# A spectral filter and a dense layer in one kernel: six rows of x by another way, the order of the first loads, three buffers, new constants

## The chip, the cores and the metric

The kernel runs on one core of a Trainium2 chip. A core has a matrix engine (TensorE, PE; its weight loads are listed as PEld), a vector engine (VectorE, DVE), a scalar engine (ScalarE, ACT), a general engine (GpSimd, POOL), and a queue engine that only issues transfers (SyncE, SP). Each works through its own queue of instructions in order and waits for others by semaphores. All transfers run on 16 DMA engines that the queues share. A transfer issued by GpSimd may change the type on the way (here fp32 to fp16); one issued by SP doesn't here. The metric is the device time of one launch in microseconds; the median of five runs is quoted.

## What is computed

```python
X = np.fft.rfft(x, axis=1)                     # x: 8 x 3008 x 256
Y = X * (filt_r + 1j * filt_i)[None, :, :]
y = np.fft.irfft(Y, n=3008, axis=1)            # the same shape
h = y.reshape(24064, 256) @ w_in               # w_in: 256 x 2048
out = np.maximum(0.01 * h, h) @ w_out          # w_out: 2048 x 256
```

A circular filter along the sequence of each batch, then two dense layers with a leaky ReLU between them. Inputs and output are fp32; matrices work in fp16 with fp32 sums.

## The kernel before

The transform of length 3008 is split as 94 x 32. `x_sb` has position n1 (94) on partitions and n2 (32) beside the 256 channels; a "row" of x below is one n2, that is 94 x 256 values. Four steps follow for each batch:

- stage 1 multiplies by `fwd1` (94-point transforms, in `small_sb`),
- stage 2 multiplies by `f2_sb`, one 128 x 128 matrix for each of 24 column groups c, and the result is multiplied with the filter (`fa_sb`, `fb_sb`),
- stage a multiplies by the inverse matrices in `small_sb`,
- stage b multiplies by `i1_sb` and leaves `yt`, channels on partitions and tokens along the row.

Between stages 1 and 2, and a and b, the data is turned. **Batch 0** does this on chip, by DVE transposes: `t1` (L376 to L379, four of them, big0 to big1) and `t2` (big2 to big0). **Batches 1 to 7** write it to DRAM (`dz1`, `dz2`) and read it back turned, on SP's queue.

Batch 0 is the start of the kernel; its order is written out by hand in the string `FIRST` (L458), one step at a time, and each engine takes its own instructions from that order. The steps:

- `warm n`: n matmuls on a zero tile (`idle`), whose result nobody uses.
- `s1p _ n0 n b`: stage 1 of n rows from row n0 into PSUM bank b; `s1e _ n0 n e`: that bank into `big[0]`, by ACT (A) or DVE (D). A bank is filled again only when it has been emptied.
- `s2p hf c n i b`: stage 2 of n column groups from c, for half hf of the channels and component i. Its product with the filter is `s2d` on DVE straight from PSUM, or `s2a` (ACT copies four groups to a spare fp32 buffer) and `s2m` (GpSimd multiplies that). Eight of the 4-group pieces go by GpSimd, the rest by DVE.
- `sap` and `sae` (ACT): stage a and its eviction; `sbp` and `sbe`: stage b and its eviction to `yt`.
- `i1`: a DVE memset of two elements of `i1_sb`, then the SP load of the whole tile. The load waits for the memset, so that it is issued when DVE has come to this place.
- `x`: GpSimd loads x of batch 1 in two halves, with w_out between them.

Ahead of that string stand the first transfers (L205 to L217). SP: `small_sb`, and thirds 1 and 0 of `f2_sb` (column groups 8 to 15, and 0 to 7; 256 KB each). GpSimd, casting to fp16: x of batch 0 in parts of 10, 10, 8 and 4 rows; the filters' first half of channels (four transfers); third 2 of f2; the filters' second half; w_in.

After batch 0 a planner sets the order. Time is counted in slots: a chunk of 512 tokens takes SL = 8 slots, its 16 first-layer products (`moe1`, L502) stand 0.5 slots apart, and the second layer of the chunk before (`plain`, L627, for three chunks, then the seven-product form at L566) lies between them. Work of the next batches is put in at times given by `PLANS`: start and spacing of stage 1 (L250), of stages 2 (L299) and a (L321) with a lag, of stage b (L342), and of the loads of x; two groups are at least `GAP` = 0.6 slots apart. These stages now have two PSUM banks between them (L486 takes the third away), so that a group waits until the one two before it has been evicted.

In stage 2 of batches 1 to 7 (`s2_group`) DVE makes two fp32 products, p1 (L311) and p2 (L308); two SP transfers swap the halves of p2 into p3, and GpSimd adds p1 and p3 (L314). For every second group of batch 1 DVE writes p3 itself (L305, L306). p1, p2 and p3 come from the pool `scr` with two buffers each; the spare buffers of batch 0 are the same ones. `AFTER` gives the delays in slots at which dependent instructions are put into their queues, `TWICE` the times of six DVE copies that make `fb_sb` and the doubled `fa_sb` (L660 to L662), `F2T` that of a load of other matrices into `f2_sb`, `SUMS` those of DVE sums for the seven-product form, `REST` those of six stage-b groups of batch 0 that are left over, `DUE` and `LEAD` limits for stage b and for the reads of turned data. In batch 1, of four stage-1 groups DVE evicts three and ACT the fourth (L642).

Of the kernel before, what the change touches and what calls it, by code (L numbers as in the profile page):

```python
# [75 lines left out]
def kernel(  # L76
# [9 lines left out]
    nc = tc.nc  # L86
    B, N, D = x.shape
# [25 lines left out]
    PLANS = (
# [14 lines left out]
    f2_sb = cpool.tile([P, NC, P], FP16, name="f2_sb")  # L128
# [10 lines left out]

    gtp = ctx.enter_context(tc.tile_pool(name="gtp", bufs=2))  # L140
    drp = ctx.enter_context(tc.tile_pool(name="drp", bufs=1, space=bass.MemoryType.DRAM))
    scrp = ctx.enter_context(tc.tile_pool(name="scr", bufs=2))
    ypp = ctx.enter_context(tc.tile_pool(name="ypp", bufs=4))
    outp = ctx.enter_context(tc.tile_pool(name="outst", bufs=4))
    psp = ctx.enter_context(tc.tile_pool(name="psp", bufs=1, space=bass.MemoryType.PSUM))
# [42 lines left out]
    def x_load(b, n0=0, nn=N2, d0=0, dn=D):  # L188

        for lo, cnt in ((0, R1),) if b + 1 < B else ((0, 64), (64, N1 - 64)):  # L190
            nc.gpsimd.dma_start(
                x_sb[lo : lo + cnt, ds(n0, nn), ds(d0, dn)],
                bass.AP(tensor=x.tensor, offset=x.offset + (b * N + lo * N2 + n0) * D + d0,
                        ap=[[N2 * D, cnt], [D, nn], [1, dn]]))
# [50 lines left out]
    def s1_group(b, g, copy):  # L245
        def go():
# [109 lines left out]
    engine = {"A": act, "D": dve}  # L356
# [91 lines left out]
        nc.vector.memset(i1_sb[:, 0, 0:2], 0.0)  # L448
        nc.sync.dma_start(i1_sb[:], i1_d.ap())

    def load_x():

        x_load(1, 0, N2 // 2)
        nc.gpsimd.dma_start(w_out_sb[:], moe_w_out.rearrange("(ct p) d -> p ct d", p=P))
# [3 lines left out]
    FIRST = """  # L458
        warm 18, s1p 0 0 2 b0, s1e 0 0 2 A, s1p 0 2 4 b3, s1p 0 6 4 b4, s1e 0 2 4 D, warm 4, s1p 0 16 4 b3,
        s1e 0 16 4 D, s1p 0 10 2 b1, s1e 0 6 4 A, s1p 0 12 4 b4, s1e 0 10 2 A, warm 2, s1p 0 24 2 b2,  # L460
        s1e 0 12 4 A, s1e 0 24 2 D, s1p 0 20 4 b3, s1e 0 20 4 A, s1p 0 26 2 b0, s1p 0 28 2 b1,
        s1p 0 30 2 b2, s1e 0 26 2 D, s1e 0 28 2 A, s1e 0 30 2 D, t1 1, t1 0, warm 14, s2p 0 0 4 0 b0,
        s2p 0 0 4 1 b1, s2p 0 16 4 0 b2, t1 2, t1 3, s2a 0 0 4 0, s2m 0 0 4 0, s2a 0 0 4 1, s2p 0 16 4 1 b0,
        s2p 0 8 8 0 b4, s2p 0 8 8 1 b3, s2a 0 16 4 0, s2m 0 16 4 0, s2a 0 16 4 1, s2m 0 16 4 1,
        s2p 0 4 4 0 b1, s2d 0 8 8 0, s2p 0 20 4 1 b2, s2d 0 8 8 1, i1, s2d 0 4 4 0, s2p 0 4 4 1 b0,
        s2p 1 8 8 0 b4, s2d 0 4 4 1, warm 1, s2p 1 8 8 1 b3, s2a 1 8 8 0, s2m 0 0 4 1, sap 0 8 b1,
        s2a 1 12 8 0, s2p 1 16 8 0 b4, s2d 0 20 4 1, sap 0 16 b0, s2m 1 12 8 0, x, s2a 1 8 8 1, s2m 1 8 8 1,
        s2d 1 16 8 0, sae 0 8 A, s2a 1 12 8 1, sae 0 16 A, s2p 0 20 4 0 b2, sap 0 4 b1, s2m 1 12 8 1,
        s2p 1 16 8 1 b3, sap 0 0 b0, s2p 1 0 8 1 b4, s2d 0 20 4 0, s2d 1 16 8 1, sae 0 4 A, s2m 1 8 8 0,
        sae 0 0 A, sap 0 20 b1, s2d 1 0 8 1, sap 0 12 b2, s2p 1 0 8 0 b3, sap 1 16 b0, sae 0 20 A,  # L470
        sae 0 12 A, sap 1 12 b1, s2d 1 0 8 0, sap 1 20 b2, t2 0, sap 1 8 b4, t2 1, sae 1 16 A, sap 1 4 b0,
        sap 1 0 b3, sae 1 12 A, warm 5, sbp 0 1 b1, sae 1 20 A, sae 1 8 A, sbp 0 4 b2, sae 1 4 A, sae 1 0 A,
        t2 3, sbp 0 5 b4, sbe 0 1 A, sbp 0 2 b0, t2 2, sbe 0 4 A, sbp 0 6 b3, sbe 0 5 A, sbp 0 7 b1,
        sbp 0 0 b2, sbp 0 3 b4, sbe 0 6 A, sbp 1 1 b3, sbe 0 0 D, sbe 0 2 A, sbp 1 0 b0, sbe 0 3 A,
        sbe 0 7 A, sbe 1 1 D, sbe 1 0 A
    """
# [180 lines left out]
    for i in range(2):  # L657
        k1s = ts(i, NC // 2)
        for n, f in enumerate((
                lambda v=k1s: nc.vector.tensor_scalar(fb_sb[64:P, v], fa_sb[64:P, v], -1.0, None, AL.mult),  # L660
                lambda v=k1s: dve(fb_sb[0:64, v], fa_sb[64:P, v]),
                lambda v=k1s: dve(fa_sb[64:P, v], fa_sb[0:64, v]))):  # L662
# [24 lines left out]
    while queue:  # L687
        time, n, stage, b, g, f = heapq.heappop(queue)
# [16 lines left out]
    for ci in range(NCHUNK + 1):  # L705
# [45 lines left out]
```

## Time and profile before

| what | us |
|---|---|
| median of five runs | 752.99 |
| all five | 752.58, 752.68, 752.99, 754.4, 755.68 |
| the profiled execution | 754.46 |
| its span | 752.7 |
| PE busy in the span | 738.9 (98%) |
| ACT, DVE, POOL busy | 559.0, 499.8, 163.5 |
| first product of the dense layers (L502) starts | 36.45 |
| last part of x for batch 0 is waited for until | 13.1 |
| first DVE transpose starts | 14.76 |

The profile has the program on one time axis that begins with the span. The granted clock of PE is full throughout (0.999). A line of the chain of waits has a start, a length, and who worked. A line of the timeline has a start, a length, engine, line, operation, result and operands with shapes, the count, and in brackets how long the engine had been idle before and what ended that. "SPq" is SP issuing a transfer; its moving of data comes later and is told by the packet records: queue, start, duration and bytes of each. A matmul's end is modelled, so steps between starts are the better measure of PE.

The 16 DMA engines are busy for nine tenths or more from about 2 us until 48 us; GpSimd's queue carries 7.47 MB of the 12.21 MB in the first 60 us.

### The profile page before, as it was taken

Reading aid. Unit: us, or ns where it says so; the run is one execution under the profiler, and the core shown is the slowest. Engines: PE = TensorE matmul, PEld = TensorE weight load, DVE = VectorE, ACT = ScalarE, POOL = GpSimd, SP = SyncE. Lnnn points to the kernel's source line nnn. Section 1 sums busy time; section 2 is a strip of 40 time slices with the busy share of each in tenths; the row PEclk is TensorE's granted clock in tenths of the full one; section 3 lists DMA queues with packets and bytes.
Section 4 is the critical chain, followed back from the end, with each engine's and each line's share of the span. In section 5 each row is a group of like instructions: output and inputs, shape, how many; then the busy total and the mean of one; then the engine's idle time right before and its main releaser. Section 6 shows DMA issues by size and latency. Waiting matters only on the chain.

```text
span 752.7 us, 19384 instructions
## 1 busy us (share of the span) xinstructions
PE 738.9 (98%) x8016; PEld 528.8 (70%) x8016; DVE 499.8 (66%) x683; ACT 559.0 (74%) x755; POOL 163.5 (22%) x169
## 2 busy tenths in 40 slices
PE   8999999999999999999999999999999999999997
PEld 3555667767777777877778777787777777777775
DVE  5886645777667776667666756776677576465565
ACT  3675797788878777787778787887777777777662
POOL 5503330342222221221133222212212210000000
PEclk9999999999999999999999999999999999999999
DMA  9985788887886567556676555544554333111011
GB/s 189 228 220 157 181 201 235 208 186 192 228 205 161 129 189 208 133 154 153 190 177 170 146 169 168 148 132 126 145 156 119 107 107 103 52 54 54 29 52 62
DMA packets 119688, 113.34 MB, mean 151 GB/s; under 512 B 16352, under 2 KB 92768, under 8 KB 119408
## 3 DMA queue, kind: packets, MB, share of 16 engines
q1 hardware_dynamic: 104447, 95.36, 42.3%
q0 software_dynamic: 14864, 16.49, 15.9%
q8 instruction: 62, 1.02, 0.6%
q10 hardware_dynamic: 289, 0.26, 0.1%
q14 instruction: 26, 0.21, 0.1%
HBM read 57.51 MB, written 50.33 MB: 143 GB/s over the span
## 4 chain that ended last, share of the span: by engine, by line
PE 92%; DMA 4%; DVE 1%; POOL 1%; issue 1%; ACT 0%; SPq 0%; DVEq 0%; ACTq 0%; POOLq 0%
PE ph L502 42%; PE po_ps L566 18%; PE pf L566 18%; PE pf L250 3%; PE pf L342 3%; PE pf L321 2%; PE pf L299 2%; DMA f_sb<-fwd_const 1%; PE po_ps L627 1%; PE pf L627 1%; DMA dz<-big 1%; DMA x_sb<-in_x_dram 1%; DMA p_b_g<-p_b_g 1%; PE pf L433 0%; POOL prod L396 0%
## 5 line engine op out<-in xcount | busy, mean ns | idle before, releaser
L507 ACT ACTIVATE gt_c<-ph 128x1024 f16<-128x1024 f32 x376 | 385.4, 1025 | 135.0 <-PE ph L502 124.3
L502 PE MATMUL ph<-yt,w_in_sb 128*128 128x512 f16 (+7 forms) x1728 | 447.6, 352 | 0.4 <-DVE yt L332 0.4
L566 PEld LDWEIGHTS <-gt_c 128*128 128x128 f16 x2800 | 202.1, 98 | 91.1
L314 POOL TENSOR_TENSOR y_b_g<-p_b_g,p_b_g 128x512 f16<-128x512 f32 x84 | 115.3, 1373 | 418.9 <-DMA p_b_g<-p_b_g 221.4
L566 PEld LDWEIGHTS <-big 128*128 128x128 f16 x2128 | 151.2, 98 | 61.6 <-issue 0.2
L502 PEld LDWEIGHTS <-w_in_sb 128*128 128x128 f16 x1728 | 137.4, 98 | 20.9 <-issue 1.8
L308 DVE TENSOR_TENSOR p_b_g<-pf,fb_sb 128x512 f32<-128x512 f32 x78 | 53.7, 688 | 32.7 <-PE pf L299 15.6
L566 PE MATMUL po_ps<-wt_sb,gt_c 128*128 128x128 f16 x704 | 70.1, 219 | 0.0
L566 PE MATMUL pf<-wt_sb,gt_c 128*128 128x128 f16 x688 | 68.5, 220 | 0.0
L566 PE MATMUL pf<-w_out_sb,gt_c 128*128 128x128 f16 x720 | 68.0, 220 | 0.0
L566 PE MATMUL po_ps<-wt_sb,big 128*128 128x128 f16 x720 | 67.5, 219 | 0.0
L566 PE MATMUL pf<-wt_sb,big 128*128 128x128 f16 x704 | 67.3, 219 | 0.0
L253 ACT CAST big<-pf 128x512 f16<-128x512 f32 x100 | 58.3, 588 | 11.9 <-PE pf L250 10.5
L566 PE MATMUL po_ps<-w_out_sb,gt_c 128*128 128x128 f16 x688 | 66.1, 220 | 0.0
L332 ACT CAST yt<-pf 128x376 f16<-128x376 f32 x120 | 56.4, 473 | 12.3 <-PE pf L342 9.0
L539 DVE TENSOR_TENSOR big<-gt_c 128x2048 f16<-128x2048 f16 (+1 forms) x46 | 58.2, 1266 | 0.1
L311 DVE TENSOR_TENSOR p_b_g<-pf,fa_sb 128x512 f32<-128x512 f32 x84 | 57.3, 682 | 1.4 <-POOL y_b_g L314 1.2
L539 DVE TENSOR_TENSOR gt_c<-gt_c 128x2048 f16<-128x2048 f16 x43 | 54.8, 1275 | 1.0
L539 DVE TENSOR_TENSOR big<-gt_c,big 128x2048 f16<-128x2048 f16 (+1 forms) x45 | 54.7, 1216 | 0.0
L539 DVE TENSOR_TENSOR big<-big,gt_c 128x2048 f16<-128x2048 f16 (+1 forms) x45 | 54.5, 1211 | 0.1
L323 ACT CAST big<-pf 128x512 f16<-128x512 f32 x84 | 49.0, 584 | 5.8 <-PE pf L321 4.1
L250 PE MATMUL pf<-x_sb,small_sb 94*128 94x512 f16 x112 | 42.7, 382 | 0.8 <-DVE big L253 0.8
(85 smaller groups left out, 618.4 us busy)
## 6 DMA issues: line engine op xcount, KB each, us to landing
dz<-big SPq DMA_DIRECT2D x98, 256.0 KB
p_b_g<-p_b_g SPq DMA_DIRECT2D x156, 128.0 KB
out_dram<-ost_c_h SPq DMA_DIRECT2D x119, 128.0 KB
big<-dz SPq DMA_DIRECT2D x42, 256.0 KB
big<-dz SPq DMA_DIRECT2D x56, 192.0 KB
x_sb<-in_x_dram POOLq DMA_DIRECT2D x41, 192.0 KB, 4.3
x_sb<-in_x_dram POOLq DMA_DIRECT2D x2, 768.0 KB, 12.2
w_in_sb<-in_moe_w_in_dram POOLq DMA_DIRECT2D x1, 1024.0 KB, 13.2
```

What stands on the lines that cost most here:

```text
L250: nc.tensor.matmul(ps, fwd1[:N1], x_sb[:N1, ds(2 * g, 2), :], start=True, stop=True)
L253: copy(st[:, ds(2 * (g % 2), 2), :], ps)
L308: nc.vector.tensor_tensor(p2[:], ps, fb, AL.mult)
L311: nc.vector.tensor_tensor(p1[:], ps, fa, AL.mult)
L314: ("y", b, g), lambda: nc.gpsimd.tensor_tensor(y1[:], p1[:], p3[:], AL.add)))
L323: nc.scalar.copy(st2[h % 4][:, ds(2 * (g % 2), 2), :], ps)
L332: copy(yv, ps.rearrange("p c a -> p a c"))
L342: nc.tensor.matmul(ps[:, j, :], z2[h % 4][:K4, j, ts(dt, P)], i1_sb[:K4, 4 * h + j, :], start=True, stop=True)
L502: nc.tensor.matmul(ph[:, j, ds(t - ci * CH, e - t)], w_in_sb[:, dt, ts(ct, P)], yt[:, dt, ds(t % N, e - t)], start=(dt == 0), stop=(dt == ...
L507: nc.scalar.activation(gts[ci][:, ds(2 * g, 2), :], ph, AF.Lrelu)
L539: nc.vector.tensor_tensor(*(v[:, ds(c0, n)] for v in (o, i0, i1)), op)
L566: nc.tensor.matmul(po[:, t], a()[:, c, ts(t, P)], w[:, c, :], start=(c == 0), stop=(c == NCH - 1))
```

## The change

- SP's first transfers are `small_sb` and then six rows of x in fp32, into the memory of `big[1]`, which is otherwise first written by `t1`. Two copies at the start of `FIRST` (`xc 0 4 A`, `xc 4 2 D`) round them to fp16 into `x_sb`. GpSimd loads the other 26 rows in parts of 10, 10 and 6.
- Third 0 of f2 is GpSimd's, behind x and ahead of the filters. Thirds 1 and 2 become steps `f2 1` and `f2 2`: a DVE memset and an SP load, as `i1` is; they stand among the evictions of stage 1 and behind the first transpose.
- `x` is split in `x 0`, `x 1` and `w_out`, in this order, later among GpSimd's products.
- The order of all steps of `FIRST` is another one, with other banks and another division between DVE, ACT and GpSimd (the numbers of pieces for each are the same in stage 2).
- The pool `scr` has three buffers for each of p1, p2, p3.
- Most constants of the planner are others.

```diff
-    SUMS = (0.09, 1.59, 2.35, 4)
-    REST = (5.37, 14.61, 8.86, 10.48, 23.53, 20.72)
-    DUE = (3.52, 0.66)
-    TWICE = (1.43, 1.84)
-    F2T = 3.24
-    LEAD = (3.85, 7.37)
-    AFTER = (0.53, 0.8, 1.33, 3.17, 0.39, 0.52)
+    SUMS = (0.05, 0.99, 2.69, 4.18)
+    REST = (4.12, 14.62, 8.89, 9.51, 23.97, 20.76)
+    DUE = (3.59, 0.63)
+    TWICE = (2.2, 2.35)
+    F2T = 3.43
+    LEAD = (3.63, 7.37)
+    AFTER = (0.53, 0.86, 1.77, 3.86, 0.39, 0.52)
...
-        (0.68, 0.31, 12.95, 0.9, 4.35, 38.33, 2.78, 7.78, 1.61),
-        (12.19, 1.53, 42.87, 2.62, 7.4, 85.59, 2.85, 16.13, 2.12),
-        (40.7, 1.73, 77.28, 3.57, 5.62, 130.03, 2.65, -0.23, 2.52),
-        (63.95, 2.85, 119.86, 3.87, 7.04, 177.42, 2.92, 12.93, 2.24),
+        (0.68, 0.42, 12.95, 0.9, 4.25, 38.32, 2.79, 7.58, 1.59),
+        (12.21, 1.53, 43.08, 2.51, 7.4, 85.59, 2.85, 16.73, 2.23),
+        (40.7, 1.74, 76.94, 3.44, 5.42, 128.19, 2.64, 0.06, 2.61),
+        (64.12, 2.86, 119.86, 3.87, 7.04, 177.42, 2.92, 13.96, 2.21),
...
-    scrp = ctx.enter_context(tc.tile_pool(name="scr", bufs=2))
+    scrp = ctx.enter_context(tc.tile_pool(name="scr", bufs=3))
...
+    EARLY = 6
+    x_early = big[1][:].bitcast(FP32)[:, : EARLY * D].rearrange("p (n d) -> p n d", n=EARLY)
     nc.sync.dma_start(small_sb[:], small_d.ap())
-    for i in (1, 0):
-        nc.sync.dma_start(f2_sb[:, ts(i, NC // FP), :], f2_d.ap()[i])
-    first_parts = ((0, 10), (10, 10), (20, 8), (28, 4))
-    for n0, nn in first_parts:
+    nc.sync.dma_start(x_early[:R1], bass.AP(tensor=x.tensor, offset=x.offset, ap=[[N2 * D, R1], [D, EARLY], [1, D]]))
+    for n0, nn in ((6, 10), (16, 10), (26, 6)):
         x_load(0, n0, nn)
+    nc.gpsimd.dma_start(f2_sb[:, : NC // FP, :], f2_d.ap()[0])
     for hf in range(2):
 
         filt_load(0, filt_r, hf * DH, DH)
         filt_load(64, filt_i, hf * DH, DH)
-        if hf == 0:
-            nc.gpsimd.dma_start(f2_sb[:, ts(2, NC // FP), :], f2_d.ap()[2])
...
+    def load_f2(i):
+
+        nc.vector.memset(f2_sb[:, i * NC // FP, 0:2], 0.0)
+        nc.sync.dma_start(f2_sb[:, ts(i, NC // FP), :], f2_d.ap()[i])
...
-        x_load(1, 0, N2 // 2)
+    def load_x(half):
+        x_load(1, half * N2 // 2, N2 // 2)
+        issued.add(("x", 1, 0))
+
+    def load_w_out():
         nc.gpsimd.dma_start(w_out_sb[:], moe_w_out.rearrange("(ct p) d -> p ct d", p=P))
-        x_load(1, N2 // 2, N2 // 2)
-        issued.add(("x", 1, 0))
+
+    def round_x(n0, n, e):
+        engine[e](x_sb[:N1, ds(n0, n), :], x_early[:N1, ds(n0, n), :])
...
+        xc 0 4 A, xc 4 2 D, warm 18, s1p 0 0 4 b3, s1p 0 4 2 b0, warm 3, s1p 0 14 2 b1, s1e 0 4 2 D,
+        s1e 0 0 4 A, s1p 0 10 4 b4, s1e 0 10 4 A, s1p 0 6 4 b3, s1e 0 14 2 D, warm 4, s1p 0 20 4 b4,
+        s1e 0 6 4 D, s1p 0 16 4 b3, s1e 0 16 4 A, s1p 0 26 2 b2, s1p 0 24 2 b0, s1e 0 24 2 A, f2 1,
+        s1e 0 20 4 D, s1p 0 28 2 b1, s1p 0 30 2 b4, s1e 0 26 2 D, s1e 0 30 2 A, s1e 0 28 2 D, t1 0, f2 2, t1 1,
+        warm 14, s2p 0 0 4 0 b3, s2p 0 0 4 1 b2, warm 2, s2p 0 8 4 1 b0, s2a 0 0 4 0, s2a 0 0 4 1, t1 3,
+        s2p 0 12 4 1 b4, t1 2, s2d 0 8 4 1, s2p 0 12 4 0 b1, s2p 0 16 8 0 b3, s2m 0 0 4 0, s2m 0 0 4 1,
+        s2d 0 16 8 0, s2a 0 12 4 1, s2p 0 8 4 0 b2, s2p 1 16 8 0 b4, s2p 0 4 4 1 b0, s2a 0 12 4 0, s2d 0 8 4 0,
...
+        x 0, s2m 1 16 8 0, sae 1 20 A, s2m 1 16 8 1, x 1, w_out, sae 1 12 A, sae 1 8 A, sap 1 16 b3,
+        sae 1 16 A, sap 1 4 b2, t2 1, sae 1 4 A, sap 1 0 b4, t2 0, sae 1 0 A, warm 4, sbp 0 1 b1, sbp 0 4 b0,
...
```

More of the change, by code (lines that the diff above doesn't have):

```diff
@@ L449, in load_i1 @@
         nc.sync.dma_start(i1_sb[:], i1_d.ap())
-    def load_x():
-        x_load(1, 0, N2 // 2)
+    def load_f2(i):
[5 more added lines that the diff above has]
+    def load_w_out():
         nc.gpsimd.dma_start(w_out_sb[:], moe_w_out.rearrange("(ct p) d -> p ct d", p=P))
-        x_load(1, N2 // 2, N2 // 2)
-        issued.add(("x", 1, 0))
+    def round_x(n0, n, e):
+        engine[e](x_sb[:N1, ds(n0, n), :], x_early[:N1, ds(n0, n), :])
@@ L458 @@
     FIRST = """
[L459 to L473, printed above, removed]
@@ L474 @@
-        sbp 0 0 b2, sbp 0 3 b4, sbe 0 6 A, sbp 1 1 b3, sbe 0 0 D, sbe 0 2 A, sbp 1 0 b0, sbe 0 3 A,
-        sbe 0 7 A, sbe 1 1 D, sbe 1 0 A
+        xc 0 4 A, xc 4 2 D, warm 18, s1p 0 0 4 b3, s1p 0 4 2 b0, warm 3, s1p 0 14 2 b1, s1e 0 4 2 D,
+        s1e 0 0 4 A, s1p 0 10 4 b4, s1e 0 10 4 A, s1p 0 6 4 b3, s1e 0 14 2 D, warm 4, s1p 0 20 4 b4,
+        s1e 0 6 4 D, s1p 0 16 4 b3, s1e 0 16 4 A, s1p 0 26 2 b2, s1p 0 24 2 b0, s1e 0 24 2 A, f2 1,
+        s1e 0 20 4 D, s1p 0 28 2 b1, s1p 0 30 2 b4, s1e 0 26 2 D, s1e 0 30 2 A, s1e 0 28 2 D, t1 0, f2 2, t1 1,
@@ new lines @@
+        warm 14, s2p 0 0 4 0 b3, s2p 0 0 4 1 b2, warm 2, s2p 0 8 4 1 b0, s2a 0 0 4 0, s2a 0 0 4 1, t1 3,
+        s2p 0 12 4 1 b4, t1 2, s2d 0 8 4 1, s2p 0 12 4 0 b1, s2p 0 16 8 0 b3, s2m 0 0 4 0, s2m 0 0 4 1,
+        s2d 0 16 8 0, s2a 0 12 4 1, s2p 0 8 4 0 b2, s2p 1 16 8 0 b4, s2p 0 4 4 1 b0, s2a 0 12 4 0, s2d 0 8 4 0,
+        s2a 1 16 8 0, s2p 0 4 4 0 b1, s2p 1 16 8 1 b3, i1, s2d 0 4 4 0, s2a 1 20 8 0, sap 0 8 b2, s2d 0 4 4 1,
+        s2a 1 16 8 1, s2a 1 20 8 1, s2m 0 12 4 0, s2p 0 16 8 1 b4, sap 0 0 b1, s2p 1 0 8 1 b3, s2m 0 12 4 1,
@@ new lines @@
+        sap 0 12 b0, s2m 1 20 8 0, sae 0 8 A, s2d 0 16 8 1, sae 0 0 A, s2p 1 8 8 1 b4, sap 0 4 b2, s2d 1 0 8 1,
+        sap 0 16 b1, sae 0 12 A, s2p 1 8 8 0 b3, sap 0 20 b0, s2d 1 8 8 1, s2m 1 20 8 1, sae 0 4 A,
+        s2d 1 8 8 0, s2p 1 0 8 0 b4, sae 0 16 A, sap 1 20 b2, s2d 1 0 8 0, sap 1 12 b1, sae 0 20 A, sap 1 8 b0,
+        x 0, s2m 1 16 8 0, sae 1 20 A, s2m 1 16 8 1, x 1, w_out, sae 1 12 A, sae 1 8 A, sap 1 16 b3,
+        sae 1 16 A, sap 1 4 b2, t2 1, sae 1 4 A, sap 1 0 b4, t2 0, sae 1 0 A, warm 4, sbp 0 1 b1, sbp 0 4 b0,
@@ L476 @@
+        sbp 0 0 b3, sbp 0 3 b2, t2 3, sbe 0 1 A, sbe 0 4 A, sbe 0 0 A, sbp 0 2 b4, sbp 0 7 b1, sbp 0 6 b0,
+        t2 2, sbe 0 2 A, sbe 0 7 A, sbp 0 5 b3, sbp 1 0 b4, sbp 1 1 b1, sbe 0 6 A, sbe 0 5 A, sbe 1 1 A,
+        sbe 0 3 D, sbe 1 0 D
     """
     steps = dict(s1p=s1p, s1e=s1e, t1=t1, s2p=s2p, s2d=s2d, s2a=s2a, s2m=s2m, sap=sap, sae=sae, t2=t2,
-                 sbp=sbp, sbe=sbe, i1=load_i1, x=load_x, warm=keep_warm)
+                 sbp=sbp, sbe=sbe, i1=load_i1, f2=load_f2, x=load_x, w_out=load_w_out,
+                 xc=round_x, warm=keep_warm)
```

## The prediction, made before the changed kernel was run

> **What bounds the kernel now.** I read the chain of waits first. TensorE (PE) holds 92% of the span, and it follows the batches: from the first product of the dense layers (L502, 36.45 us) to the end, PE is the path. To see what it loses there I took the start of every matmul in the trace and compared the step to the next one with the median step of its form. After 36.45 us the excess is 5.15 us in all, and from 150 us on nothing. So a change like this can win in two places: in the first 36.45 us, where PE mostly waits, and in those 5.15 us. The chain up to there:
>
> ```profile
> PE 92%; DMA 4%; DVE 1%; POOL 1%; issue 1%; ACT 0%; SPq 0%; DVEq 0%; ACTq 0%; POOLq 0%
> 1.24 6.57 DMA x_sb<-in_x_dram
> 8.09 11.01 DMA f_sb<-fwd_const
> 24.83 0.59 POOL x_sb L191
> 25.43 1.17 POOL w_out_sb L454
> 27.13 3.41 POOL prod L396 x3
> 36.45 1.06 PE ph L502 x4
> ```
>
> The reader sees three transfers on it (x, then the third part of f2 that is queued behind x and half the filters, 11.01 us) and three GpSimd DMA issues ahead of GpSimd's last filter products. But one engine goes through this stage almost without a pause: VectorE (DVE), in the timeline:
>
> ```profile
> 14.76 4.62 DVE L379 STREAM_TRANSPOSE big<-big 128x1024 f32<-128x1024 f32 x4
> 20.51 2.36 DVE L396 TENSOR_TENSOR prod<-ph,fa_sb 128x1024 f16<-128x1024 f32 x2 [1.12 <-PE ph L388]
> 29.96 2.36 DVE L425 STREAM_TRANSPOSE big<-big 128x1024 f32<-128x1024 f32 x2
> 32.87 2.37 DVE L425 STREAM_TRANSPOSE big<-big 128x1024 f32<-128x1024 f32 x2 [0.55 <-ACT big L419]
> 22.91 0.32 SPq L449 DMA_DIRECT2D i_sb<-inv_const  x1
> ```
>
> (The last line is SP's, used below.) DVE's idle time in brackets is 1.12 us (waiting for the f2 third) and 0.55 us (waiting for ACT, which waited for GpSimd). The prologue is therefore the DVE sum: 14.76 + 4.62 + 1.13 + ten products 9.45 (20.51 to 29.96) + 2.36 + 0.55 + 2.37, 35.24, and 1.21 from there to L502. Later, in batch 1:
>
> ```profile
> 39.13 0.96 DVE L660 TENSOR_SCALAR fb_sb<-fa_sb 64x3072 f16<-64x3072 f16 x1
> 40.12 0.69 DVE L253 CAST big<-pf 128x512 f16<-128x512 f32 x1
> 40.87 0.38 PE L250 MATMUL pf<-x_sb,small_sb 94*128 94x512 f16 x1 [0.32 <-DVE big L253]
> 72.88 0.69 DVE L311 TENSOR_TENSOR p_b_g<-pf,fa_sb 128x512 f32<-128x512 f32 x1 [0.61 <-POOL y_b_g L314]
> 73.62 0.38 PE L321 MATMUL pf<-y_b_g,small_sb 128*128 128x512 f16 x1 [0.72 <-DVE p_b_g L311]
> 105.43 6.73 DMA dz<-big
> ```
>
> By the steps, PE loses 0.49 + 0.67 at 40 and 42.6 us (an eviction stuck behind a filter copy), 1.14 at 67.6, 0.89 at 72.6 (p1 waits for GpSimd to free its buffer) and 1.47 at 113.6 (the spectra of batch 1 on their way through DRAM): 4.66 of the 5.15.
>
> **The change, part by part.**
>
> *x.* SP's second DMA is now six rows of x in fp32 (96 packets of 6,144 bytes) in place of two f2 thirds; GpSimd's casting loads shrink from 32 to 26 rows. In the packet records f2 took 256 packets x 97 ns = 1.55 us of the 16 engines; the new one, by i1's packets of 6,016 bytes (232 ns), 96 x 0.232 / 16 = 1.4. From its first packet (f2's first: 2.67) it runs alone until GpSimd's first (3.34), then in turn with those (445 ns): three packets an engine alone, three at 0.68, landing near 6.3. At worst all six share: 2.67 + 4.05 + 1.0 = 7.7. Rounding costs 1.06 on ACT (L279's 128x1024 row) and 0.69 on DVE (its 128x512 row): nothing while the 18 idle matmuls run, which end at 7.92 as before; without that cover, in the worst case, 0.9. GpSimd's x is six rows of packets shorter (by its ten-row packets 0.6 x 0.445 x 96 / 16 = 1.6 us), so x is in at about 11.4 instead of 13.1. But DVE and ACT evict it: on DVE 2, 2, 4, 4, 2, 2 rows from 8.77, 4 x 0.69 + 2 x 1.22 = 5.2, 14.0 with no gap; on ACT the last three blocks follow a bank that DVE frees at 11.7: product at 12.4, then 1.06 + 0.62 + 0.62, 14.6. So the transposes start at 14.6 (14.3 to 15.7): **0.15** gained, though the data is 1.7 us earlier.
>
> *f2.* Its first third follows x on GpSimd's queue; 64 packets of 163 ns end by 11, needed at 17. The second is asked for when DVE gets to a 0.06 us memset at about 11.7, needed at 18.1; the third behind the first transpose, at 14.6 + 1.16 + 0.06 = 15.8. It is needed when DVE has done its first product: 14.6 + 4.62 + 0.06 + 0.6 = 19.9, less 0.67 for PE (19.84 to 20.51 in the trace): 19.2. SP has nothing ahead of it. When it lands the trace does not show. From below: SP's first DMA had its first packet 0.62 after its issue ended (1.11 to 1.73); 15.8 + 0.35 + 0.62 + 8 x 0.097 + 0.95 to landing = 18.5, no wait. From above: i1, issued in the same way into the same queue, had its first packet only at 26.06, 2.83 after its issue; and 256 f2 packets took 5.5 us beside x, so 128 take 2.75: 15.8 + 0.35 + 2.83 + 2.75 + 0.95 = 22.7, a wait of 3.5. i1's excess of 2.2 us is some seven of the 0.325 us packets of w_in that it met; here filter packets of 41 ns stand in the way, so I take seven of these, 0.3: landing at 15.8 + 0.35 + 0.62 + 0.3 + 8 x (0.097 + 0.041) + 0.95 = 19.1, and put down a wait of **0.3** for 1.12. Behind it in PE's queue stand the products for four GpSimd multiplications, which would be late by as much.
>
> The Trainium skill ("DMA: Bandwidth & Descriptors", section "Queues, rings and completion order") has an engine drain 9 to 17 descriptors of one ring before it turns to the next. For i1 that would be 2.9 to 5.5 us; the trace has 2.2. For the f2 third it would be 0.4 to 0.7 instead of my 0.3, and the time 0.1 to 0.4 longer. A rule against the change stands in the same page's section "SWDGE vs HWDGE vs iDMA": a two-port DVE copy locks GpSimd out of the rings it writes, and the rounding on DVE is such a copy amid GpSimd's issues; no row here shows it, and by 0.69 us at most it would delay filters, not x.
>
> *Order of GpSimd.* Of its three issues (0.59 + 1.17 + 0.53 us ahead of three products) only x 0 stays ahead of the last two; they end 1.7 earlier, near 28.8. ACT's wait of **0.55** goes with it; late next is ACT itself (12 copies of 0.6 from 23.5: 30.7, for a need at 31.4). w_out now lands behind both halves of x: before, w_out and x took 27.9 to 41; in the new order w_out's 6.5 us end near 42, needed by L627 at 48.3 - 1.5. That cover is some 4 us; past it each us costs one.
>
> *Constants.* Batch 1's first-stage groups keep their slots, for GAP 0.6 exceeds both 0.31 and 0.42 (0.68 + 0.6 g). The six filter copies move from 1.43 + 1.84 n to 2.2 + 2.35 n: 2.2, 4.55, 6.9 and 9.25 lie each beside a group that ACT evicts (g = 3, 7, 11, 15 at 2.48, 4.88, 7.28, 9.68), where DVE has room; before, 1.43 and 3.27 stood ahead of DVE's own evictions. **1.16** goes (0 to 1.16).
>
> *Three buffers.* p1 at 72.88 would not wait 0.61: **0.6** of the 0.89 (0 to 2.0, if the 1.14 went too; but that one follows three DVE products of 0.69 in a row and has no buffer wait). The 1.47 of batch 1's spectra keeps its slots; 0 taken, -1.0 to 1.47.
>
> *Sum.* Prologue 0.15 + 1.12 - 0.3 + 0.55 - 0.06 = 1.46 (L502 at 35.0); later 1.76; together 3.2. Against the profiled execution (754.46, span 752.7 and 1.76 around it) that is 751.2. The median of the runs is 1.47 below that execution, and the sum carries over: 752.99 - 3.2 = **749.8**. A measurement tells about 0.3%, 2.26 us, so faster means under 750.73, slower over 755.25.
>
> **Rivals.** *The wait is only replaced*: f2's last third comes as i1 did, 1.9 to 3.5 us late, and the prologue gives nothing or loses up to 1.8. For it: i1's row, the nearest by queue. Against: it met long packets. With a loss of 0.7 the constants and buffers remain: 752.99 + 0.7 - 1.76 = 751.9, no measurable change. *More than forecast*: the 1.47 stall goes too, as DMA traffic shifts: 748.3. For it, 6.73 us for one 256 KB write; against, nothing in the change is aimed at it. *Slower*: the f2 third takes what the third on GpSimd's queue took in this trace, 11.0 us, for the filters fill the engines: 15.8 + 11.0 = 26.8, DVE idle 26.8 + 0.67 - 19.9 = 7.6 instead of 1.12; 752.99 + 7.6 - (0.15 + 1.12 + 0.55 - 0.06) - 1.76 = 757.1. It decides from a landing at 25 on (19.2 and a wait of 5.8). Against: that one had two us of filters and part of x ahead in its own queue.
>
> **How the numbers follow.** Forecast 0.48, only replaced 0.27, more 0.10, slower 0.15. Faster is forecast and more, 0.58; same 0.27; slower 0.15. The range takes in the 1.47 with no f2 wait (748.0) and, upward, a 3.5 us wait with a late first eviction (753.9); the slower rival is left out.
>
> **What would show it.** First L502 near 35.0, transposes at 14.6, DVE's idle before its second product under 0.5, none before the third inverse transpose; no PE step over 0.4 between 36 and 45 us; a shorter one near 71. I am wrong if the third of f2 lands after 21, if x in fp32 lands after 7, or if PE waits for w_out at L627.

## The result, and the profile after

The changed kernel takes 754.49 us (median of 23 runs, 752.87 to 757.39), the kernel before 753.08 in the same comparisons (43 runs). The ratio is 1.002, with a 95% interval of 1.0011 to 1.0028: **slower by 0.2%**, some 1.4 us, where 3.2 us less had been forecast, and outside the range. By the marks that the prediction set itself (faster under 750.73, slower over 755.25) it is neither. In the second set of runs of the changed kernel (a2 below) one run took 2,730 us and is left out of the ratio. The profiled execution has a span of 753.1 us (752.7 before). What PE loses, by the steps between matmul starts as in the prediction:

| us | before | after |
|---|---|---|
| first product of the dense layers | 36.45 | 37.76 |
| PE's excess from there on | 5.15 | 4.76 |
| of it at 40 and 43 us (evictions, batch 1) | 1.16 | none |
| at 67 to 68 us | 1.14 | 1.11 |
| at 72 us (buffer of p1) | 0.89 | none |
| at 113 us (spectra of batch 1) | 1.47 | none |
| at 166 us | none | 0.90 |
| at 207 us | none | 1.56 |

So the start lost 1.3 us where it should have won 1.5, and the steady part, where three stalls did go, grew two others. Together that is 0.9 us lost; the rest of the span differs by up to 0.8 us between profiles. (The second profile of the changed kernel, a2 below, has the first product at 36.42, as before, and an excess of 5.97: 0.8 lost.) From the chain of waits of the changed kernel, in order of time, in that start:

```profile
12.21 2.12 ACT big L279 x3
14.36 1.27 DVE big L379 x2
15.64 5.34 DMA f_sb<-fwd_const
21.03 0.63 PE ph L388 x8
24.53 0.97 PE pf L416 x2
32.15 2.29 DVE big L425 x2
34.98 2.74 ACT yt L332 x7
```

The third of f2, 11.01 us on the chain before, is on it again with 5.34: asked for at 15.64, landed at 20.98. DVE's timeline of the same kernel (not all rows) has what came of it:

```profile
14.36 2.42 DVE L379 STREAM_TRANSPOSE big<-big 128x1024 f32<-128x1024 f32 x2 [0.20 <-ACT big L279]
18.95 0.65 DVE L396 TENSOR_TENSOR prod<-pf,fa_sb 128x512 f16<-128x512 f32 x1
21.76 1.22 DVE L396 TENSOR_TENSOR prod<-ph,fa_sb 128x1024 f16<-128x1024 f32 x1 [2.16 <-PE ph L388]
26.22 5.93 DVE L396 TENSOR_TENSOR prod<-ph,fa_sb 128x1024 f16<-128x1024 f32 x5 [1.29 <-ACT big L419]
32.06 4.71 DVE L425 STREAM_TRANSPOSE big<-big 128x1024 f32<-128x1024 f32 x4
```

The transposes begin at 14.36, as forecast or better, and the 0.55 before the third inverse transpose is gone, as forecast. But DVE waits 2.16 us before its second product, where 1.12 had stood before its first and 0.3 was forecast, and then 1.29 more. That second gap goes with TensorE's clock, as a2 below bears out. In the table of stretches (busy time and, third from the end, the granted clock):

```profile
core 0: us, PE busy (x) PEld busy (x) DVE busy (x) ACT busy (x) POOL busy (x), PEclk, DMA share, GB/s
18.50:21.00 2.50, 0.57 (x14) 0.30 (x8) 1.10 (x2) 1.07 (x2) 2.50 (x3) 1.00 1.60 232
22.00:25.00 3.00, 3.00 (x36) 1.86 (x33) 2.88 (x5) 1.46 (x3) 1.67 (x2) 0.52 1.09 217
```

PE stood idle for most of 18.5 to 21 us, waiting for f2, and from 22.1 us its clock was halved for 3.4 us, so that the products that DVE needed next came late.

At 166 us, the timeline of the changed kernel, GpSimd, DVE and PE:

```profile
163.33 1.27 POOL L314 TENSOR_TENSOR y_b_g<-p_b_g,p_b_g 128x512 f16<-128x512 f32 x1 [1.13 <-DMA p_b_g<-p_b_g]
163.39 2.29 DVE L548 TENSOR_TENSOR big<-gt_c 128x2048 f16<-128x2048 f16 x1
166.93 0.38 PE L250 MATMUL pf<-x_sb,small_sb 94*128 94x512 f16 x1 [0.74 <-DVE p_b_g L311]
```

A DVE sum for the seven-product form, 1.22 us as a rule, took 2.29 beside a GpSimd addition that had begun 0.06 us earlier; DVE's next two products were late by as much, and PE waited for the bank that they read.

At 207 us, first SP's issues and then GpSimd and PE:

```profile
198.92 2.04 SPq L269 DMA_DIRECT2D big<-dz  x4
201.07 0.55 SPq L309 DMA_DIRECT2D p_b_g<-p_b_g  x1
201.77 0.51 SPq L310 DMA_DIRECT2D p_b_g<-p_b_g  x1
207.41 1.26 POOL L314 TENSOR_TENSOR y_b_g<-p_b_g,p_b_g 128x512 f16<-128x512 f32 x1 [9.98 <-PE po_ps L575]
208.72 0.38 PE L321 MATMUL pf<-y_b_g,small_sb 128*128 128x512 f16 x1 [1.40 <-POOL y_b_g L314]
```

and SP's issues in the kernel before:

```profile
199.96 1.19 SPq L309 DMA_DIRECT2D p_b_g<-p_b_g  x1
201.20 0.59 SPq L310 DMA_DIRECT2D p_b_g<-p_b_g  x1
202.50 1.74 SPq L269 DMA_DIRECT2D big<-dz  x4
```

Before, the two swaps of a group of batch 3 went ahead of the four reads of batch 2's turned spectra (192 KB each); now they stand behind them, GpSimd's addition waits for p3, and PE for the addition. (The addition waits for several things, and its row names the one that came last by the profile; in the second profile of the changed kernel the same row, at 207.26, is idle for 9.24 and ended by the swap's transfer.) The constants say so. A read is put in at the last stage-a group of its batch + AFTER[4] + LANDED, and a swap AFTER[1] behind its group. Working the planner through, for the reads and for the second group of batch 3: before, reads at 79.09 + 0.39 + 2.43 = 81.91 slots and swaps at 80.85 + 0.8 = 81.65; after, reads at 78.25 + 0.39 + 2.43 = 81.07 and swaps at 80.77 + 0.86 = 81.63.

### The profile page after: what moved, and what is told of

Same layout as the page of the kernel before. It is cut to its first block, busy times and chain, and to the rows that moved or that the text cites. A ratio compares the mean times of both kernels' runs of the same rounds, so it can differ in the third digit from the quotient of the medians.

```text
span 753.1 us, 19396 instructions
## 1 busy us (share of the span) xinstructions
PE 739.5 (98%) x8017; PEld 529.2 (70%) x8017; DVE 503.5 (67%) x687; ACT 560.2 (74%) x755; POOL 161.7 (21%) x168
## 4 chain that ended last, share of the span: by engine, by line
PE 95%; DVE 2%; DMA 1%; ACT 1%; issue 0%; POOL 0%; SPq 0%; DVEq 0%
PE ph L511 43%; PE po_ps L575 18%; PE pf L575 18%; PE pf L250 3%; PE pf L342 3%; PE pf L321 2%; PE pf L299 2%; PE pf L636 1%; PE po_ps L636 1%; DMA big<-in_x_dram 1%; DMA f_sb<-fwd_const 1%; DVE big L548 0%; PE pf L416 0%; PE ph L392 0%; ACT yt L332 0%; PE pf L433 0%
## 5 line engine op out<-in xcount | busy, mean ns | idle before, releaser
L314 POOL TENSOR_TENSOR y_b_g<-p_b_g,p_b_g 128x512 f16<-128x512 f32 x84 | 113.7, 1354 | 422.0 <-DMA p_b_g<-p_b_g 249.0
L548 DVE TENSOR_TENSOR gt_c<-gt_c 128x2048 f16<-128x2048 f16 x43 | 56.5, 1315 | 1.1
```

Of the source, the lines that this page charges most:

```text
L314: ("y", b, g), lambda: nc.gpsimd.tensor_tensor(y1[:], p1[:], p3[:], AL.add)))
L548: nc.vector.tensor_tensor(*(v[:, ds(c0, n)] for v in (o, i0, i1)), op)
```

## The experiments

Times are medians; the ratio is to the kernel before, run beside them, with its interval. "First product" and "excess" are of the one profiled execution, and vary from one to the next: the start of e2 stands unchanged in e8 and e13, whose first products are at 33.95, 34.67 and 35.67, and that of the kernel before in e5, e7 and e14 (36.45, 36.21, 36.13, 35.34). A difference of 1 us in that column shows nothing by itself. e1, e3, e10, e12 and e15 are edits of the changed kernel, a2 is the changed kernel again, e5, e7 and e14 are edits of the kernel before, and e8, e9, e11 and e16 are edits of e2; e13 is an edit of e8.

| kernel | us | ratio (95%) | first product | excess |
|---|---|---|---|---|
| e1_f2_early | 751.71 | 0.9979 (0.9965 to 0.9993) | 34.56 | 4.81 |
| e2_f2_pool | 751.81 | 0.9977 (0.9964 to 0.9989) | 33.95 | 4.87 |
| e3_old_consts | 753.71 | 1.0003 (0.9991 to 1.0014) | 36.36 | 4.91 |
| e7_before_both | 754.12 | 1.0008 (0.9991 to 1.0026) | 36.13 | 5.67 |
| e8_z2_later | 750.34 | 0.9952 (0.9935 to 0.9968) | 34.67 | 4.89 |
| e9_no_fp32_x | 752.97 | 0.9986 (0.997 to 1.0001) | 34.03 | 4.78 |
| e5_before_three_bufs | 753.04 | 0.9985 (0.9971 to 1.0) | 36.21 | 4.96 |
| a2_after_again | 755.2 | 1.0009 (0.9992 to 1.0025) | 36.42 | 5.97 |
| e12_warm_wait | 756.82 | 1.0037 (1.0022 to 1.0052) | 35.83 | 7.85 |
| e11_issues_ahead | 752.99 | 0.9987 (0.9978 to 0.9997) | 34.97 | 5.65 |
| e13_old_sums | 751.36 | 0.9964 (0.9951 to 0.9978) | 35.67 | 5.21 |
| e14_before_both_z2_later | 752.04 | 0.9975 (0.996 to 0.999) | 35.34 | 2.42 |
| e15_after_z2_later | 753.64 | 0.9996 (0.9981 to 1.0012) | 37.30 | 4.25 |
| e16_warm_no_wait | 754.45 | 1.0005 (0.9993 to 1.0016) | 35.57 | 6.32 |

### The late third of f2: e1, e2

```diff
-        s1e 0 20 4 D, s1p 0 28 2 b1, s1p 0 30 2 b4, s1e 0 26 2 D, s1e 0 30 2 A, s1e 0 28 2 D, t1 0, f2 2, t1 1,
+        f2 2, s1e 0 20 4 D, s1p 0 28 2 b1, s1p 0 30 2 b4, s1e 0 26 2 D, s1e 0 30 2 A, s1e 0 28 2 D, t1 0, t1 1,
```

> Changed kernel with the step f2 2 moved from behind the first transpose to directly behind f2 1, so that the last third of f2 is asked for near 11.7 us instead of 15.64. Theory (the late third is what costs): it lands before 18.5 us, DVE's idle time before its second filter product falls from 2.16 to under 0.4 us and the later gap of 1.29 goes too, the first L511 moves from 37.76 to 34.6-35.8, and the time falls by 2 to 3 us against the changed kernel (about 751.5 to 752.5, ratio to before 0.998 to 0.9995). Rival (the start is not passed on, the new constants cost the time): L511 is as early, but the time stays within 0.5 us of the changed kernel's, ratio to before 1.001 to 1.003.

```diff
+        if hf == 0:
+            nc.gpsimd.dma_start(f2_sb[:, ts(2, NC // FP), :], f2_d.ap()[2])
...
-        s1e 0 20 4 D, s1p 0 28 2 b1, s1p 0 30 2 b4, s1e 0 26 2 D, s1e 0 30 2 A, s1e 0 28 2 D, t1 0, f2 2, t1 1,
+        s1e 0 20 4 D, s1p 0 28 2 b1, s1p 0 30 2 b4, s1e 0 26 2 D, s1e 0 30 2 A, s1e 0 28 2 D, t1 0, t1 1,
```

> Changed kernel with the last third of f2 loaded by GpSimd between the two halves of the filters, as the kernel before does, and nothing else moved. Theory: GpSimd's queue holds six rows of x less ahead of it, it lands near 18.5-19 us, DVE's idle time before its second product is 0 to 0.5 us, first L511 at 35 to 36, time 1.5 to 2.5 us under the changed kernel's. Rival (SP's queue is not slow, the third is late because the 16 DMA engines are full): it lands near 21 us here too and nothing changes.

Both are faster than the changed kernel and than the kernel before; first products at 34.56 and 33.95 stand even ahead of the 35.0 that the prediction had for the change itself. From DVE's timeline in e2:

```profile
14.03 4.62 DVE L381 STREAM_TRANSPOSE big<-big 128x1024 f32<-128x1024 f32 x4 [0.28 <-ACT big L281]
18.58 0.65 DVE L398 TENSOR_TENSOR prod<-pf,fa_sb 128x512 f16<-128x512 f32 x1
19.25 1.23 DVE L398 TENSOR_TENSOR prod<-ph,fa_sb 128x1024 f16<-128x1024 f32 x1
22.41 5.93 DVE L398 TENSOR_TENSOR prod<-ph,fa_sb 128x1024 f16<-128x1024 f32 x5
28.26 4.71 DVE L427 STREAM_TRANSPOSE big<-big 128x1024 f32<-128x1024 f32 x4
```

No gap before the second product and none behind it. The rival of e1, that the start is not passed on, falls: 1.9 to 3.8 us of start, depending on which two profiles are compared, come out as 2.7 us of median (751.71 and 751.81 to 754.49). The rival of e2 falls too: on the same full engines the third lands at 18.20 when GpSimd's queue has it from 8.42 us on. It was late for when and on which queue it was asked for. In time by a narrow margin, though: in the five other kernels with e2's way it lands between 18.18 and 19.73, and in e13, the latest, DVE waits 0.94 for it.

### How long a request waits: e10

```diff
-    for hf in range(2):
-        filt_load(0, filt_r, hf * DH, DH)
-        filt_load(64, filt_i, hf * DH, DH)
+    filt_load(0, filt_r, 0, D)
+    filt_load(64, filt_i, 0, D)
```

> Changed kernel with the filters loaded whole, in four transfers of 512-byte packets in place of eight of 256-byte ones; the requests for the thirds of f2 stay where they are. It measures how long a request on SP's queue waits for its first packet while GpSimd's queue is full: 3.55 us behind 256-byte packets in the changed kernel (0.6 on quiet engines), 2.3-2.8 behind 4,096-byte ones. If a fixed number of bytes stands ahead (about 30 KB an engine, as 7 packets of 4,096 and some 128 of 256 would be): first packet of f2 1 3 to 4 us after its issue. If a fixed number of packets (128): over 5 us. If it is the time in GpSimd's queue turn, as my 7 packets in the prediction: under 1.5 us.

The second third was issued by 12.09 us and had its first packet at 15.28: 3.19 us, behind packets of 512 bytes. The last one waited 3.21. (One execution, 759.92 us; the filters' first half comes later here, and DVE waits 3.72 us for it, so the time means nothing for the change.) With the rest of the packet records:

| request on SP's queue | GpSimd's packets | of them, to one engine in the wait | issue's end to first packet, us |
|---|---|---|---|
| some 30 requests after 500 us in each of three profiles (before, after, e2), SP's queue quiet and no packet of GpSimd's about | none | 0 | 0.53 to 0.67 |
| thirds of f2, changed kernel (two) | 256 bytes | 154, 134 | 3.55, 3.55 |
| the first such request of the 11 other runs with it | 256 bytes | | 3.51 to 3.79 |
| thirds of f2, e10 (two) | 512 bytes | 46, 33 | 3.19, 3.21 |
| i1, before and after | 4,096 bytes | 9, 7 | 2.83, 2.26 |
| i1, the 14 other runs but e10 | 4,096 bytes, in some 256 first | | 2.31 to 3.07 |

In e10 i1 was asked for when GpSimd's queue moved next to nothing (4 packets in all during the wait), and waited 0.62. So a request waits when that queue is full, and about as long behind small packets as behind large ones: it isn't a number of packets, and the prediction's seven of 41 ns, 0.3 us, were a tenth of it. Counted in bytes, GpSimd's queue moved 30 to 40 KB an engine in each of these waits; less the share of the quiet 0.62, 28 to 33 KB in the rows shown but one (2.26, 22 KB). That a fixed number of bytes stands ahead fits, and so does a time of about 3 us; what holds them isn't shown.

### Clock: a2, e12, e16

> The changed kernel once more, as the base of this set and for a second profile of it. In the first profile TensorE's granted clock fell to half from 22.1 to about 25 us, behind its wait of 2.1 us for the third of f2, and DVE then waited 1.29; in e3_old_consts the same wait of 2.2 us was not followed by that. If the half clock belongs to the wait and comes in some executions only, this profile has it or not, and first L511 stands at 37.8 or at 36.4; the time within 0.5 us of 754.5.

The second profile has the same wait (2.15) and no half clock; the stretch that read 0.52 reads 1.00:

```profile
22.00:25.00 3.00, 2.98 (x54) 1.90 (x50) 2.85 (x6) 2.34 (x5) 1.70 (x3) 1.00 1.06 216
```

Its first product is at 36.42, 1.3 us earlier than in the first. Of the four profiles with this wait (the changed kernel twice, e3, e15) two have the half clock, and e10, with longer waits, has it too; none of the other kernels has it between the first 7 us and the last matmul.

The traces say which. In all 17 profiles every change of the clock lies a whole number of periods of 3.413 us behind the first on record, the rise to the full clock (in the changed kernel 5.03 us; the half clock from 22.10 to 25.51 is 5 and 6 periods behind it): the clock seems to be set anew at the end of each, and where the periods lie differs from one execution to the next. Counting how long PE was busy in each, the period ahead of the half clock has 1.46 us (changed kernel), 1.46 (e15) and 1.13 (e10, where the next has 1.59 and the clock stays halved for another). In a2 a period ended in the middle of the same wait, and the two that share it have 2.21 and 2.48. At full clock, no period of any profile up to its last matmul has less than 1.55 (e3).

So the wait's price is 1.0 us more than before on DVE, always, and some 1.3 on top where most of it falls into one period. The mean granted clock of all runs agrees: the profiles with the half clock at the start have 0.997 or less, the others 0.998 or more. Of the 57 runs of kernels with this wait 28 are at 0.997 or less; of the 121 runs of kernels without it 7, of the kernel before 6 of 119. In the changed kernel it is 12 of 23, with a median of 754.99 against 753.86 for the 11 others; in a2 4 of 11 (755.72 and 754.13), in e15 8 of 12 (754.18 and 752.60), in e3 4 of 11 (753.88 and 753.66). About half of the executions thus pay for the clock, some 0.2 to 1.6 us by these medians.

```diff
-        s2p 0 12 4 1 b4, t1 2, s2d 0 8 4 1, s2p 0 12 4 0 b1, s2p 0 16 8 0 b3, s2m 0 0 4 0, s2m 0 0 4 1,
+        s2p 0 12 4 1 b4, t1 2, s2d 0 8 4 1, s2p 0 12 4 0 b1, warm 8, s2p 0 16 8 0 b3, s2m 0 0 4 0, s2m 0 0 4 1,
```

> Changed kernel with eight more idle matmuls (warm 8, 1.7 us at full clock) ahead of the stage-2 products that wait for the last third of f2. Theory (the wait's second half of the price is TensorE's clock): the wait itself stays at 2 us on DVE, no half clock behind it, no second gap of 1.29, first L511 at 36.3-36.6 in its profile, median 0.3 to 1.3 us under the changed kernel's of this set. Rival (the clock has no part in the median): same time within 0.3 us.

The median went the other way: 756.82 beside 755.2. The profile has what was expected of the start (no half clock, DVE's gap 2.15, first product 35.83), and an excess of 7.85 after it: 1.77 at 111, 1.82 at 207 and 1.12 at 221 us. The matmuls keep PE busy through the wait (no period under 2.8 us there), but the clock's share of the median is not shown by this.

> Kernel e2_f2_pool with the eight idle matmuls of e12 at the same place, where there is hardly a wait to fill. If idle matmuls there cost time by themselves (1.7 us of PE's queue ahead of the products that DVE waits for, in part beside the wait): first L511 0.5 to 1.6 us later than 33.95, time 0.5 to 1.6 us over e2_f2_pool. If e12 was slow for what comes later in the run: L511 as said, but the time up by more than that, and PE's excess after it grows.

The same eight matmuls where nothing waits: DVE idle for 1.81 before its second product (none in e2), first product 35.57, 1.6 later than in e2, and 2.6 us on the median, more than the start explains. Here too a step of 1.11 comes at 219 us (the one of 1.92 at 205 is e2's 1.74 at 203). Idle matmuls ahead of products that DVE needs are not free. For e12 that is not shown: its start is no later than a2's, and its 1.77 at 111 us isn't in e16. Why the step at 219 to 221 us is in just these two stays open.

### Constants and buffers: e3, e5, e7

```diff
+    SUMS = (0.09, 1.59, 2.35, 4)
+    TWICE = (1.43, 1.84)
+    LEAD = (3.85, 7.37)
...
```

> Changed kernel with all planner constants of the kernel before (SUMS to PLANS), three buffers kept. Theory: the start stays at L511 37.8; PE loses the two steps at about 41 and 43 us again (0.49 and 0.67), so 0.5 to 1.5 us slower than the changed kernel, ratio to before 1.0025 to 1.004. Rival (the new constants cost the time): 1 us or more faster than the changed kernel, ratio 0.9995 to 1.0015.

Slower was expected, and by the ratio it isn't (1.0003; the changed kernel 1.002 and 1.0009). The steps at 40 and 43 us are back (0.56 + 0.67), the one at 113 with 1.06, and those at 166 and 207 are gone: an excess of 4.91 for 4.76. The rival is nearer: the new constants are worth nothing here. The step at 113 us comes and goes by itself: with the new constants it is 0 in the changed kernel, 0.91 in e8 and 1.77 in e12.

```diff
-    scrp = ctx.enter_context(tc.tile_pool(name="scr", bufs=2))
+    scrp = ctx.enter_context(tc.tile_pool(name="scr", bufs=3))
```

> Kernel before with three buffers in scr and nothing else. Theory (the wait of p1 for a buffer at 72.9 us was worth 0.6): the PE step of 0.89 at 72.6 us falls under 0.4, the one of 1.14 at 67.6 stays, time 0.3 to 0.9 us less, ratio 0.9988 to 0.9997. Rival (the buffer comes free as late through GpSimd's order): both steps stay, ratio 0.9995 to 1.0005.

As the theory had it: the step of 0.89 is gone, the one at 67 us stays with 1.11, and the ratio is 0.9985, though its interval reaches 1.0.

> Kernel before with the new constants and three buffers alone, its start untouched. Theory (their gain of 1.76 us was rightly predicted and is only covered by the start): L502 at 36.4, PE's excess after it 5.15 less 1.2 to 2, ratio to before 0.997 to 0.9985. Rival: new stalls of about the same size take the place of the old ones later, as at 166 and 207 us in the changed kernel, ratio 0.9993 to 1.001.

The edit is the one of e5 and all constants of the changed kernel, in the kernel before. The steps at 40, 43 and 72 us go, the one at 113 falls to 0.32, and 0.78 at 165, 2.01 at 206 and 0.47 at 203 us come: excess 5.67, ratio 1.0008. The rival holds.

### The reads ahead of the swaps: e8, e14, e15

```diff
-    LEAD = (3.63, 7.37)
+    LEAD = (3.63, 3.8)
```

> Kernel e2_f2_pool with one constant changed: LEAD's second value 3.8 for 7.37, which puts the four reads of batch 2's turned spectra at slot 81.79 instead of 81.07, behind the two swaps of batch 3's second group (81.63) on SP's queue. Theory (the PE stall of 1.5-1.7 us at 203-207 us is those swaps waiting behind four reads of 192 KB): the stall falls under 0.4 us, nothing of its size comes elsewhere, and the time falls by 1 to 1.7 us against e2_f2_pool, ratio to before 0.9955 to 0.997. Rival (GpSimd's own queue or the sum on DVE holds the group up): the stall stays over 1 us, ratio 0.997 to 0.999.

> Kernel e7_before_both (the kernel before with new constants and three buffers) with LEAD's second value at 3.8. Theory (the 1.76 us I forecast for constants and buffers were real and were given back at 206 us, where two swaps stand behind four reads): PE's step of 2.0 at 206 us goes, ratio to before 0.996 to 0.9985 where e7 had 1.0008. Rival (the steady part is full of such meetings and another takes its place): ratio 0.9995 to 1.0015.

> Changed kernel with LEAD's second value at 3.8 and its late third of f2 kept. Theory: step at 206 us (1.6 and 2.4 in two profiles) under 0.4, time 1 to 2 us under the changed kernel's 754.5-755.2, ratio to before 0.9985 to 1.0003; with e2 and e8 this gives each of the two failed terms alone. Rival: 1.001 to 1.003.

The step at 203 to 207 us is gone in e8 and e14, with SP's issues in the old order again. In e14:

```profile
195.78 0.54 SPq L309 DMA_DIRECT2D p_b_g<-p_b_g  x1
196.37 0.59 SPq L310 DMA_DIRECT2D p_b_g<-p_b_g  x1
197.01 2.08 SPq L269 DMA_DIRECT2D big<-dz  x4
```

The same edit is in all three, in e8 on top of e2, in e14 on top of e7, in e15 alone. e14 is what the prediction had in mind: constants and buffers alone, in the kernel before, with the one meeting removed, give 0.9975, 1.9 us of 753.59 (0.8 to 3.0 by the interval), and an excess of 2.42. In e15 the swaps' step went and a step of 1.35 at the reads themselves (L342, 204 us) came in this profile, with the half clock at 21 us; the ratio is 0.9996 all the same. e13, with the same constant, has such a step too (1.24 at 202 us): reads that are put off can come too late. e8 is the fastest kernel of the study, 0.9952, and beats both. Its profile has another step of 0.87 at 363 us, where the constant moved the reads of batch 4 too; e13 has the same, e14 and e15 haven't.

### x in fp32 and GpSimd's order: e9, e11; the sums: e13

```diff
-    nc.sync.dma_start(x_early[:R1], bass.AP(tensor=x.tensor, offset=x.offset, ap=[[N2 * D, R1], [D, EARLY], [1, D]]))
-    for n0, nn in ((6, 10), (16, 10), (26, 6)):
+    for n0, nn in ((0, 6), (6, 10), (16, 10), (26, 6)):
...
-        xc 0 4 A, xc 4 2 D, warm 18, s1p 0 0 4 b3, s1p 0 4 2 b0, warm 3, s1p 0 14 2 b1, s1e 0 4 2 D,
+        warm 18, s1p 0 0 4 b3, s1p 0 4 2 b0, warm 3, s1p 0 14 2 b1, s1e 0 4 2 D,
```

> Kernel e2_f2_pool with all 32 rows of x cast by GpSimd again, in parts of 6, 10, 10 and 6, and without the two rounding copies. Theory (six rows in fp32 shorten GpSimd's queue by 1.6 us, but evictions bound the stage): the first transpose moves from 14.03 to 14.7-15.7, first L511 from 33.95 to 34.6-35.7, time 0.5 to 1.7 us over e2_f2_pool. Rival (evictions hide it all): transposes under 0.3 us later, time within 0.4 us.

The first transpose begins at 13.73 (14.03 in e2) and the first product is at 34.03 (33.95): the rival's side in the profile. The median is 1.2 us higher (the profiled execution is the fastest of the twelve), but the two intervals overlap. No gain of the fp32 rows is shown.

```diff
-        sap 0 12 b0, s2m 1 20 8 0, sae 0 8 A, s2d 0 16 8 1, sae 0 0 A, s2p 1 8 8 1 b4, sap 0 4 b2, s2d 1 0 8 1,
+        sap 0 12 b0, s2m 1 20 8 0, x 0, w_out, x 1, sae 0 8 A, s2d 0 16 8 1, sae 0 0 A, s2p 1 8 8 1 b4, sap 0 4 b2, s2d 1 0 8 1,
...
-        x 0, s2m 1 16 8 0, sae 1 20 A, s2m 1 16 8 1, x 1, w_out, sae 1 12 A, sae 1 8 A, sap 1 16 b3,
+        s2m 1 16 8 0, sae 1 20 A, s2m 1 16 8 1, sae 1 12 A, sae 1 8 A, sap 1 16 b3,
```

> Kernel e2_f2_pool with GpSimd's three issues (x 0, w_out, x 1; 0.6 + 1.2 + 0.6 us) put back ahead of its last two filter products. Theory: those products end 1.8 us later, ACT and then DVE wait 0.5 to 1.2 us before the third inverse transpose, first L511 34.5 to 35.2 instead of 33.95, time 0.4 to 1.2 us over e2_f2_pool (751.8). Rival (another engine is late by then anyway): L511 under 34.3.

The wait before the third inverse transpose is back with 0.48. The first product is 1.0 later, no more than between executions of one start, and the median 1.2 us over e2's, with intervals that overlap: what the wait costs isn't shown.

```diff
-    SUMS = (0.05, 0.99, 2.69, 4.18)
+    SUMS = (0.09, 1.59, 2.35, 4)
```

> Kernel e8_z2_later with SUMS of the kernel before. The PE stall of 0.8-0.9 us near 163-166 us stands behind a DVE sum that took 2.29 us instead of 1.22 beside a GpSimd addition. Theory (the sums' new slots brought the two together): that step goes, PE's excess between 150 and 200 us under 0.2, time 0.3 to 0.9 us under e8_z2_later, ratio to before 0.994 to 0.9955. Rival: it is GpSimd's slot (AFTER) that moved; the step stays and the time with it.

The step at 163 to 166 us is gone in this profile, but it is gone in e14 and e15 too, with the new sums, and the median is not lower than e8's (751.36 to 750.34). By the run alone this is open, but the traces settle what the step is. The 11 profiles that have it (0.75 to 0.90) are those in which that sum takes 2.14 us or more because a GpSimd addition was already running; in the six others it takes 1.21 to 1.64. In e14 the two meet as well, but the sum came first by 0.04 us: it took 1.22, the addition 2.31, and there is no step. (e13's own sums begin 0.05 ahead of their addition, with the same result.) So the new constants brought the two together, and a few hundredths of a us decide which of them waits.

## Why the prediction was wrong

**The third of f2** is the step that failed first: "so I take seven of these, 0.3", which gave a landing at 19.1 and a wait of 0.3. The packets that i1 met were counted, and their number was carried over to shorter ones. What carries over is the time, or the bytes: 3.55 us from issue to first packet, landing at 20.98, and a wait of 2.16. The upper bound of the same paragraph, taken from i1's 2.83 us, had up to 3.5, and i1's was called "the nearest by queue" among the rivals; the choice between the ends was wrong, not the ends. The 11.0 us of the rival "slower" were too much: the request took 5.34. On GpSimd's queue the third does take that long (9.8 us in e2), but there it is asked for at 8.42. The page of the Trainium skill that was weighed ("DMA: Bandwidth & Descriptors", "Queues, rings and completion order", typically 9 to 17 descriptors to a turn) would have made it, by the prediction's estimate, 0.4 to 0.7 for these packets; the measured 2.9 above the quiet 0.6 doesn't agree.

**What was not in the sum**: TensorE's clock. The prediction let PE's wait of 2 us cost what it lasts. In the profiled execution 1.29 us of DVE's time came on top; in two of four profiles with that wait, and by the mean clock in about half of the runs, the clock was halved.

**Constants and buffers, 1.76.** The terms were right: the 1.16 at 40 and 43 us are gone in every kernel with the new TWICE but e11 (one step of 0.67 there), the buffer's 0.89 in every one with three buffers, and e14 has 1.9 us for them. The sum was wrong, because the prediction asked for batch 1 only which groups keep their slots. For batch 2 the reads moved by 0.84 slots, past the two swaps of batch 3, and 1.49 to 2.42 us were lost there in each of the ten profiles with the new constants and LEAD as it was; nothing in the diff names it. The DVE sum that met a GpSimd addition lost another 0.75 to 0.90. Neither loss had a term in the prediction.

**x, evictions, GpSimd's order** were right in the main. The six fp32 rows landed at 6.53 for 6.3, the last of x at 12.41 (11.65 in a2) for 11.4, the transposes began at 14.36 for 14.6 (the terms of that sum give 14.7), and there is no stall for w_out at L636. That the 0.55 is gone in the changed kernel says little, since DVE came 2 us later there; with DVE in time it is gone in e2, back with 0.48 in e11, and stands with 0.38 and 0.39 in e1 and e9. That the earlier data of x is worth little was right and still too kind: e9 has nothing for the fp32 rows.

**The rivals.** "The wait is only replaced" is what happened in the start, with a loss of 1.3 in the first profile that lies within its "up to 1.8", and none in the second. It was priced at 751.9 because the 1.76 were taken off. No rival had the steady part give its gain back, though the 1.47 had been noted as a thing that could turn either way.

## What to carry to other kernels

A transfer that is asked for "when an engine gets there" should be priced by what an already measured request of that kind took on a full queue, in us, and asked for so much earlier; here the place of one request was worth some 2.7 us. When a schedule's constants change, look for pairs on one queue whose order turns over, in every batch and not only the one whose stalls are to go. And a wait of TensorE can cost more than it lasts, in some executions and not in others.

## What the runs showed of the hardware

- A request on SP's queue had its first packet 0.53 to 0.67 us after its issue on quiet engines and 2.3 to 3.8 us after it while GpSimd's queue was full, about as long behind packets of 256 bytes (3.55) as behind 512 (3.19).
- TensorE's granted clock changed only at whole periods of 3.413 us, in 17 profiles of 17. It was 0.5 after periods in which PE was busy for 1.46, 1.46 and 1.13 us, and stayed 1.0 after periods with 1.55 us (e3) and more. Some 2 us without work were enough if they fell into one period. (The ends of matmuls are modelled, so these sums are estimates.)
- A DVE sum of 128x2048 fp16 (1.22 us as a rule) that began at least 0.03 us into a GpSimd addition, with 0.25 us or more of it left, ended 1.08 to 1.09 us after that addition's end: 11 times in the profile before, 14 times in the one after, and in all other profiles. At 163 us the addition ran from 163.33 to 164.60, and the sum from 163.39 took 2.29. The Trainium skill ("Trainium Architecture — The Big Picture", "What this means for kernel authors") has DVE and GpSimd share a port pair under an exclusive lock; the rows agree with that, as does e14, where the sum came first and the addition took 2.31 instead of 1.27.
